# Three quarters of the query and key projection as products beside the gate's, the tokens' normalising on POOL, and a new issue table

## The chip, the core and the metric

The kernel runs on one core of one Trainium2 chip, in one launch. The metric is the device time of that core in microseconds (us), a median over runs. The core's engines are named as the profile names them: PE (TensorE matmul; PEld is its weight load), DVE (VectorE), ACT (ScalarE), POOL (GpSimd) and SP (SyncE, which here only issues DMAs).

## The reference

What is computed is a layer norm, an attention of 32 heads of width 16 without a mask, and a SwiGLU block whose output, through a SiLU, gates the attention's output; all in float32, 2048 tokens of width 512, inner width 1792.

```python
x = A_x                                     # [1, 2048, 512]
xn = _layernorm(x, axis=-1)
s = _A_ref(xn, A_wqkv, A_wo)                # qkv = xn @ wqkv; softmax(q k^T / 4) v per head; @ wo
g = _silu(_B_ref(xn, B_w1, B_w3, B_w2))     # (_silu(xn @ w1) * (xn @ w3)) @ w2
return x + s * g
```

## The kernel before

**Products in three parts.** A product in float32 precision is made of fp32r matmuls: each operand is split into a rounded high part and a rest (names ending in `h` and `l`), and three matmuls (l by h, h by l, h by h; `split3`, or `three` in the gate) are summed in PSUM. With a contraction of 512 in four slices of 128 rows (`KC`), one product of 128 by 512 outputs is 12 matmuls.

**Stage 1, the prologue** (L433 to L629). The 16 tiles of 128 tokens are normalised (`spread`: statistics on DVE and a power on POOL; `norm`: one DVE instruction), transposed on PE (`transposed`) and split by ACT and DVE into `xts`, four blocks of 512 tokens. Per block the kernel computes all eight row blocks of q and k (128 rows each: eight heads' worth; row blocks 0 to 3 are q, 4 to 7 are k), splits them (ACT copies the high part `sh`, DVE subtracts to `sl`) and stores them to DRAM (`qk`), and computes v for its four token tiles (`token_values`). For the first pair of heads, slices of k and q are loaded back into `ks` and `qs` and the first 64 maxima are taken between the products (`beside`, from a hand-written table `groups`). The normalised blocks 0 to 2 are stored to DRAM (`xt`) for the gate; block 3 stays in SBUF.

**Stage 2, the attention with the gate beside it.** The 16 pairs of heads are done in halves of 1024 queries, so 32 phases of 16 chunks (128 keys each). Four kinds of PE work are mixed:

- `m` (L403): scores of 128 queries by 512 keys for the row maxima, a matmul of 62 rows; DVE reduces it (L405). They run one phase ahead.
- `e` (L643): scores of 128 keys by 512 queries with the maximum already subtracted through two more rows; ACT takes the exponential into one of 23 `pt` tiles (L646).
- `f` (L877): the gate's products, each matmul cut into two halves of 64 rows. `m`, `e` and `f` thus all use half of the array's rows, and two of them run side by side, in two lanes.
- `pv` (L659): the values of one chunk, four matmuls side by side in column groups of the array, float32, eight records in the trace.

When a phase's maxima are complete, `max_rows` reduces and transposes them and writes them as two rows into `qs` through DMAs (L430); the phase's `e` can begin when these have landed.

**The order** of the PE work in stage 2 is the string `ORDER_OF_ISSUE`: a lower-case or capital letter is a half matmul in lane 0 or 1 (`f`, `s` for e, `m`), `v` or `r` is a chunk of values, `o` a step of the output projection. What cannot be issued at its letter by a planner (`Model`, times in us) is issued late. Weights of the gate come as `units` of 128 by 512 (`Weights`): a load into `wr`, then two POOL instructions that split it (L335, L336). SP issues all DMAs, in program order.

**Stage 3**, the output projection (`o`), begins beside the last two phases and ends the kernel.

Of the kernel before, what the change touches and what calls it, by code (L numbers as in the profile page):

```python
# [9 lines left out]
F32 = mybir.dt.float32  # L10
# [24 lines left out]
COLS = (2, 1, 0)  # L35
# [17 lines left out]
    "MffSMfSffSMfMfSffSMffSffMfsMfsMffSfsFFmFFsfMsfFmFsFFmFfSmFfFmfMFfmMvvsMSmfFFfsFfMFsFfmSfFsFmFFsfMsfF"  # L53
    "mFFffMMffMMfmMvvvMssSmFfFfFfMFsFfmSfFsFmFsFfMsfFFmSfFMffMSffsMvMsMffSfFfSFmSfFfMsfFSmFfSfFmFsFmFsFfF"
    "mFMfSfmSvMmmSmSvvMssSMmvmSFsFmFsFsFmsFFmFffFmFSfmFFfmSvfMfSfMSffSMfMfSfrMsmMsSvFmMsmMFmvvsMfSmFfFfSf"
    "MSffFmSfSfFmFsfFMFsFfmfFFMffSffMSffSfMsFFfmFsFFmsFFfmFsFmFsFMfFfMfMfmSvmSmMmFFvvMsSsmMvSmFmFssMvsMMm"
    "mSvvSmfSfMSffFfMSffMfSfFmFsFMffSsFFfmFFffMSffMfsFFFmsFsFFfmsFfFMsfFFmSfmFFfMffSMmvvmSMsMsvMmFsSmsFvm"
    "SMmMmvvRFsmFFsFmFsFsmFFffSfMfSfMfSfFFmfSffMSffMMsvmMMssSvmSFmsFfFSfFmfSFfMsFfFsMsFFfmSFffMsfFMFffMfS"
    "sMvSmMmFsFsvsMFmFsSmvSmmMmSvvmSmSmSvSmFsfMfSfFfMfSfMfSFfMfsFMffSsFFfmFFffMfSfMfsFFFmsfFFsFmFsFfMsFFf"
    "mSFfFmfMMffMsvvMmMmMmvvvMsfSfMfFSfFmSfFfSfMfFsFmfFFsfMFsMfFsFffMSfFmFfSffMSmvMssSMmvmSsSfMrSfMffSMff"  # L60
    "SfMfSfsFFmFsFfMsFFfmsFFMfsFsfFMfFsFmFsFmFsFfMfFsFFmsFFfMfMffSmSvmSSmMmvvSmMmsSvMffMMmmSvvfSfMfSfMSff"
    "MfSfSFfmFsFFfmFsFFmsFFmFfsFFmFfsFmFsFmfFSfFsFmFFfMfSfffMSMffSffMfSsMvvvvvFmFsFmsFFsmFsFFmFmFsFsFmFFf"
    "sFFfsfMfSFfMfSfMfFsFmFfFffMSfSffMfSMffMSffMSffMrvSmsMmMvvSmMsSmvsMFmFsFfsFfMFsFfmSFfsFmFsFFfmSFfFmsF"
    "sFfFmFsFfMfSFfmFFffMfSfMfSfSffMFsFfmFsFmFsFfFmFsFFmfFmFMfmMvvvmSSsmMvmSSmfSfMvSmmMsMvvmSfMfSfSfFFmfS"
    "FmFsFmFfSfMfFsFfSfMFsFfmFFffMfSfMfSffSfMFsfMfFsFmsFFfFmSfFmFsFsFfmFmFMmvvvmSSsmSvvRMsfSFfMfSfFmFsfFf"
    "SMsFFfmFsFfMsFffSMfSFfmFFffMSfffMSFfsfMsFfFmFsFmFsFFmFfsFmFSffMfFmMvvvMsfMfSFsFffMFsFfmSFfsFmFFsfMFs"
    "FfmSFfFmffMSfmMvvmSmSMsvvSmSsmMvmFFsFmFssFmFfFfSfMfSfMfSfFMfsfFMfSffSFmFFffMffMsFFfMfFsFfsFMFsFfmSFf"
    "FmsFfFmFfMfMmMvvvSmMsmMvvmSFmFsFfsFfMFsFfmSfFFsmFsFfMfSfFmSfFfMfSfMfSsvvvRsMfSFfMfsFFmFsfFFsMfSfFmfS"
    "fFMsfFfMSffSFmFFffMSffmFFsFmFsFsfFMFfsFmfSfFMsfFmFFffSMMsvvmSSssSvvSmSmSmvvMsmMmSvvMfSffMSfMffSfsFFm"
    "FFsfMsfFmFsFFmfFSmfFfFFfMfSfMfSfSffMsFFfmsFFmFsFFfmFsFFmsFFfMfMfMfmSvvMssMMmvvmSMfsFFffSfMfSfMfSfFmF"  # L70
    "sFMffSfFFsmFFsfMsFfMfSfmFFffSfMMmvvmSmSsMvvRSfMfSfMfSffMfSfSffMFsFfmSfFFmsFFsFfmFFsfMFsfFFmsFmFfSFfs"
    "FmFsFfMfSFfmSfsFfFfMfMMmvvvvMffSSmFmFfFfFsmFFssFFfMfFsFmFsFfFmSfFsFmFsFfMfSfFmsFfFMfSffMSfSfFfMffSmM"
    "vvmSMmmSvvfMfSfMSffMfSfsFFmsFfFMsfFmFSfFmFsFsfFMFsFfmSFfmFsFfFmFsMfFsFfFsFfMfSmMvvmSMmmSvvsMMmSsvvRf"
    "SfMfSfMfSfMfSffSfMFsfFmSFfFmsFsFFfmFFsFmsFfFmFFsmFFsFmFfsFsFfFSmvsMmMmSvvSmmMsMvvMsfSfMfFfSFmfSFfMsF"
    "ffSMfFsFmFsFmFsFFfmFMffSSmvvvMsfFmSfFsFfMsFFfmSfFfSmSfFfMSffFmSFfmfFFFfMffSMffSffMfSsFfFmFFsfMsFFfmF"
# [72 lines left out]
def kernel(ctx: ExitStack, tc: tile.TileContext, x, wqkv, wo, w1, w3, w2, out):  # L148
# [163 lines left out]
    class Weights:  # L312
# [37 lines left out]
        def next(self):  # L350

            i = self.taken
            self.taken += 1
            self.pump()
            return i, self.parts.pop(i)

    wts = Weights()
    for b in range(TB):
        for hf in range(HF):
            for f in range(hf * FH, (hf + 1) * FH):  # L360
                for w in (w1, w3):
                    wts.units.append(w[:, f * P:(f + 1) * P].rearrange("(k p) f -> p k f", p=P))
# [1000 lines left out]
```

## Time and profile before

| | us |
|---|---|
| median of 3 runs (lowest to highest) | 1720.81 (1720.58 to 1721.6) |
| the profiled execution | 1719.59 |
| its span, first to last instruction | 1717.8 |
| PE busy, DVE busy, ACT busy, POOL busy | 1708.2, 1408.0, 1224.0, 765.5 |
| first `f` matmul (stage 2 begins) | 160.7 |
| last chunk of values begins (stage 3 alone from there) | 1694.8 |

The durations used are those of the profiled execution, which is 1.2 us under the median; 1.8 us of its time lie outside its span. Matmuls are pipelined, so PE's busy time says only that it had something in flight; the spacing of the matmuls' starts says how much it did.

### The profile page before, as it was taken

The page shows a single profiled execution, that of the slowest core. Times are in us where ns is not written, and L with a number is a line of the kernel's source. Part 1 is how long each engine was busy: PE and PEld are TensorE (multiplying, and loading weights), DVE is VectorE, ACT ScalarE, POOL GpSimd, SP SyncE. Part 2 cuts the span into 40 slices and gives each one's busy share as a digit, 9 for nine tenths or more (in the row PEclk, how much of TensorE's full clock was granted, in tenths as well). Part 3 has the DMA queues.
Part 4 walks back from the last instruction along what each step waited for, and adds up shares of the span by engine and source line. Part 5 has one row for each costly group of instructions (what it writes and reads, how often), then busy time and mean ns, then how long its engine had stood idle before and what let it go on. Part 6 is the DMA issues. An engine that isn't in the chain of part 4 may idle for free.

```text
span 1717.8 us, 35102 instructions
## 1 busy us (share of the span) xinstructions
PE 1708.2 (99%) x13188; PEld 1102.6 (64%) x13188; DVE 1408.0 (82%) x2343; ACT 1224.0 (71%) x2440; POOL 765.5 (45%) x791
## 2 busy tenths in 40 slices
PE   9999999999999999999999999999999999999998
PEld 7877565666666666666666666666666666665456
DVE  7566999889898888888898798887988878889636
ACT  4223777777877786877777877887778777877880
POOL 3102646065635662466355643555465525653011
PEclk9999999999999999999999999999999999999999
DMA  8656203042333212222423222131513312331264
GB/s 286 245 204 204 71 22 86 21 82 70 65 104 88 62 55 51 64 60 69 100 88 62 62 67 68 43 82 54 137 51 65 74 37 71 99 85 29 81 206 147
DMA packets 146794, 155.34 MB, mean 90 GB/s; under 512 B 42304, under 2 KB 100672, under 8 KB 143648
## 3 DMA queue, kind: packets, MB, share of 16 engines
q1 hardware_dynamic: 145760, 151.52, 32.4%
q8 instruction: 104, 1.70, 0.4%
q10 hardware_dynamic: 864, 1.57, 0.2%
q14 instruction: 66, 0.54, 0.1%
HBM read 107.97 MB, written 44.02 MB: 88 GB/s over the span
## 4 chain that ended last, share of the span: by engine, by line
PE 95%; issue 2%; DMA 2%; SPq 1%; DVE 0%; ACT 0%; POOL 0%; ACTq 0%; POOLq 0%; DVEq 0%
PE f L877 28%; PE pv L659 27%; PE m L403 17%; PE e L643 15%; PE m L522 2%; PE e L197 2%; PE e L201 2%; PE e L199 2%; PE m L495 0%; PE m L418 0%; DMA ovl<-o 0%; SPq L695 0%; DMA wr<-in_A_wqkv_dram 0%; DMA ovh<-o 0%; DMA inh<-in_A_x_dram 0%
## 5 line engine op out<-in xcount | busy, mean ns | idle before, releaser
L405 DVE TENSOR_REDUCE mp<-m 128x1 f32<-128x512 f32 x2048 | 1276.8, 684 | 174.6 <-PE m L403 103.6
L646 ACT ACTIVATE pt<-e 128x512 f32<-128x512 f32 x2048 | 1061.0, 612 | 260.7 <-PE e L643 139.1
L643 PE MATMUL e<-qs,ks 64*128 64x512 f32 x2048 | 726.4, 408 | 2.5 <-DMA qs<-ml 2.5
L403 PE MATMUL m<-ks,qs 62*128 62x512 f32 x2048 | 725.6, 415 | 0.0
L659 PE MATMUL pv<-pt,vt 128*17 128x512 f32 x4096 | 489.8, 595 | 0.0
L403 PEld LDWEIGHTS m<-ks,qs 62*128 62x128 f32 x2048 | 339.1, 184 | 146.9 <-ACT pt L646 34.6
L643 PEld LDWEIGHTS e<-qs,ks 64*128 64x128 f32 x2048 | 345.1, 184 | 120.5 <-issue 35.0
L659 PEld LDWEIGHTS pv<-pt,vt 128*17 128x17 f32 x4096 | 94.2, 96 | 235.9 <-issue 229.1
L877 PE MATMUL f<-xtl,wh 64*128 64x512 f32 x488 | 177.9, 391 | 0.0
L877 PE MATMUL f<-xth,wl 64*128 64x512 f32 x488 | 176.1, 393 | 0.0
L877 PE MATMUL f<-xth,wh 64*128 64x512 f32 x488 | 174.4, 391 | 0.0
L762 POOL TENSOR_TENSOR h<-g,h 128x512 f32<-128x512 f32 x56 | 72.1, 1288 | 228.2 <-ACT h L758 228.2
L877 PE MATMUL f<-wh,hs 64*128 64x512 f32 x496 | 157.8, 393 | 0.0
L877 PE MATMUL f<-xtl,xeh 64*128 64x512 f32 x408 | 148.7, 391 | 0.0
L877 PE MATMUL f<-xth,xel 64*128 64x512 f32 x408 | 143.4, 394 | 0.0
L877 PE MATMUL f<-xth,xeh 64*128 64x512 f32 x408 | 142.6, 392 | 0.0
L877 PE MATMUL f<-xeh,hs 64*128 64x512 f32 x400 | 127.1, 392 | 0.0
L336 POOL TENSOR_TENSOR wl<-wr,wh 128x512 fp32r<-128x512 f32 x92 | 118.5, 1288 | 7.7
L335 POOL TENSOR_SCALAR wh<-wr 128x512 fp32r<-128x512 f32 x92 | 57.1, 621 | 115.9 <-PE e L643 56.5
L336 POOL TENSOR_TENSOR xel<-wr,xeh 128x512 fp32r<-128x512 f32 x76 | 97.9, 1288 | 6.3
L796 POOL TENSOR_SCALAR th<-th 128x512 f32<-128x512 f32 x16 | 9.9, 619 | 187.5 <-ACT th L792 187.5
L877 PE MATMUL f<-wl,hs 64*128 64x512 f32 x248 | 92.3, 392 | 0.0
(179 smaller groups left out, 2071.0 us busy)
## 6 DMA issues: line engine op xcount, KB each, us to landing
wr<-in_B_w_dram SPq DMA_DIRECT2D x168, 256.0 KB
qs<-qk SPq DMA_DIRECT2D x186, 64.0 KB
ks<-qk SPq DMA_DIRECT2D x90, 128.0 KB
qk<-sh SPq DMA_DIRECT2D x32, 256.0 KB
qk<-sl SPq DMA_DIRECT2D x32, 256.0 KB
v<-vrow SPq DMA_DIRECT2D x16, 272.0 KB
xin<-in_A_x_dram SPq DMA_DIRECT2D x16, 256.0 KB
g<-part SPq DMA_DIRECT2D x16, 256.0 KB
```

The source lines that it names most:

```text
L197: nc.tensor.matmul(ps, lhs[1], rhs[0], start=first, stop=False)
L199: nc.tensor.matmul(ps, lhs[0], rhs[1], start=False, stop=False)
L201: nc.tensor.matmul(ps, lhs[0], rhs[0], start=False, stop=last)
L335: nc.gpsimd.tensor_scalar(hi, t, 1.0, 1.0, op0=ALU.mult, op1=ALU.mult)
L336: nc.gpsimd.tensor_sub(lo, t, raw(hi))
L403: nc.tensor.matmul(ps, qs[p % 2][64 * h:64 * h + KM, q0:q0 + P], ks[p % 2][64 * h:64 * h + KM, c * 512:(c + 1) * 512], start=True, stop=True)
L405: nc.vector.reduce_max(mp[p, half][:, h, qt, c:c + 1], ps, axis=AX.X)
L643: nc.tensor.matmul(ps, ks[p % 2][64 * h:64 * h + KR, k * P:(k + 1) * P], qs[p % 2][64 * h:64 * h + KR, q0:q0 + 512], start=True, stop=True)
L646: done = nc.scalar.activation(pt, ps, AF.Exp, scale=DH ** -0.5)
L659: nc.tensor.matmul(pv[32 * j:32 * j + VW, :], vt[2 * p // GH][:, key, 2 * p % GH + j % 2, :], pt, start=key < 2 if last else k == 0, stop= ...
L762: nc.gpsimd.tensor_mul(h2, g, h2)
L877: nc.tensor.matmul(ps, left[r], right[r], start=starts and lane == 0, stop=ends and lane == 1)
```

## The change

Of the 32 products of the q and k projection (eight row blocks by four blocks of tokens), the prologue keeps the eight of row blocks 0 and 4, the first eight heads (`token_rows`). The other 24 become products of the gate's list: `rows_here` puts a pair of them (k, then q) ahead of gate products 0, 2 and 5 and behind the last down product of the first half (`hf == 0`) of the first three token blocks of the gate. Their tokens are the gate's current block, or another block fetched again from `xt` in DRAM into the tile `rows2` (`fetch_tokens`, `some_tokens`). Their weights are 24 more `units`, split by POOL. Their output is copied by ACT, split by POOL instead of DVE (`projected`), and stored by SP. A chunk that will need rows not yet stored is held back (`NEED`).

In the prologue, the normalising instruction of tiles 2 to 15 moves from DVE to POOL; the stores of v and of the high parts of q and k move from SP's queue to ACT's; block 3 is stored to `xt` too; the memsets stand in other places; the table `groups` is new, and 12 of the 16 last early maxima are in two groups of six. The last steps of the first phase's maxima (transposing them and writing them to `qs`) move out of the prologue into stage 2, which now begins with `m` and `f` work alone.

```diff
+    def room_between(n, hf):
+        return {0: (0, 2, 5, FH), 1: ()}[hf] if n < KC - 1 else ()
...
-            nc.sync.dma_start(v_d[t], vrow[t % 2].rearrange("p h d -> p (h d)"))
+            nc.scalar.dma_start(v_d[t], vrow[t % 2].rearrange("p h d -> p (h d)"))
...
-            nc.vector.tensor_scalar(xn, xin[t], mv[:, 0:1], rs, op0=ALU.subtract, op1=ALU.mult)
+            (nc.vector if t < 2 else nc.gpsimd).tensor_scalar(xn, xin[t], mv[:, 0:1], rs, op0=ALU.subtract, op1=ALU.mult)
...
+        def token_rows(b, c):
+            hi, lo = xts[b]
+            rbk = KC * c
+            ps = bank("e")
+            for k in range(KC):
+                run(split3(ps, [w[:, k, :] for w in wqk[c]], (hi[:, k, :], lo[:, k, :]), k == 0, k == KC - 1))
...
+            nc.scalar.copy(sh, ps)
+            nc.vector.tensor_sub(sl, ps, raw(sh))
+            cols = slice(b * 512, (b + 1) * 512)
+            nc.scalar.dma_start(raw(qk_d[rbk][0])[:, cols], raw(sh))
+            nc.sync.dma_start(raw(qk_d[rbk][1])[:, cols], raw(sl))
+
+        def more_tokens(n):
+            if n < NT:
+                transposed(n, xn.pop(n))
+                if n + 4 < NT:
+                    load_x(n + 4)
+                if n + 2 < NT:
+                    xn[n + 2] = norm(n + 2)
+
         for b in range(TB):
+            cols = slice(b * 512, (b + 1) * 512)
+            for s in range(2):
+                nc.sync.dma_start(raw(xt_d[b][s]), raw(xts[b][s]).rearrange("p k t -> p (k t)"))
+            token_rows(b, 1)
+            if b == TB - 1:
+                load_k(0, cols)
+                wts.start()
+            beside(b, 0)
+            more_tokens(4 * b + 4)
+            if b == 0:
+                nc.gpsimd.memset(*next(blank))
+                nc.gpsimd.memset(*next(blank))
+                more_tokens(5)
+            token_rows(b, 0)
...
+            beside(b, 1)
+            more_tokens(4 * b + (5 if b else 6))
+            if b == 0:
+                nc.gpsimd.memset(*next(blank))
+                nc.gpsimd.memset(*next(blank))
+                more_tokens(7)
+                load_q(0, 0, cols)
+                continue
+            for i in range(TB):
+                run(token_values(b, i))
...
+                beside(b, 2 + i)
+                if i < 2:
+                    more_tokens(4 * b + 6 + i)
...
+        def projected(ps, i, rbk, b):
+            flush(i - 1)
...
+            nc.scalar.copy(c, ps)
...
+                nc.gpsimd.tensor_scalar(sh.bitcast(F32R), c, 1.0, 1.0, op0=ALU.mult, op1=ALU.mult)
+                nc.gpsimd.tensor_sub(c, c, sh)
...
+                    nc.sync.dma_start(raw(qk_d[rbk][s])[:, b * 512:(b + 1) * 512], v)
...
+                def rows_here():
+                    t = rest.pop(0)
+                    src = xt if t == b else rows2
+                    for c in (1, 0):
+                        some_tokens()
+                        i, w = wts.next()
+                        mms = [m for k in range(KC) for m in three([v[:, k, :] for v in w], [v[:, k, :] for v in src])]
...
-    ready = {0: 0.5}
+    ready = {}
...
-    rows, outs = [], []
+    rows, outs = [[2.0, first_rows, 2, 0]], []
```

The table grows from 8617 to 9194 letters, 576 of them more `f` and `F`; one row of it before and one now:

```diff
-    "MffSMfSffSMfMfSffSMffSffMfsMfsMffSfsFFmFFsfMsfFmFsFFmFfSmFfFmfMFfmMvvsMSmfFFfsFfMFsFfmSfFsFmFFsfMsfF"
+    "MfMfMffMMffMMffMffMffRfMffMfMffMmFfFFmFffFfFFfFFfFmFmFfffMffMffMfSFfFfsFFfFsfFFsmFFsFmFFffmFsFFmFsfF"
```

Counted over the whole order of PE, there are 4032 half matmuls `f` before and 4608 now, and 384 full matmuls of the q and k projection before (lines L197 to L201) and 96 now; `m`, `e` and the records of `pv` are 2048 each before and now. The values stand in runs of chunks with no other matmul between them: 259 runs before (85 of one chunk, 119 of two, 37 of three, 12 of four, 6 of five), 204 now (32, 82, 54, 26, 10).

On PE, in the third phase (`e` and `m` of the second and third pair of heads; `x4` at a `pv` row is one chunk), before:

```order
L659 MATMUL pv<-pt,vt 17x512 x4
L643 MATMUL e<-qs_132,ks_134 128x512
L403 MATMUL m<-ks_135,qs_133 128x512
L877 MATMUL f<-xth,wh_1929 128x512
L403 MATMUL m<-ks_135,qs_133 128x512
L877 MATMUL f<-xth,wl_1930 128x512
L643 MATMUL e<-qs_132,ks_134 128x512 x2
L403 MATMUL m<-ks_135,qs_133 128x512
L659 MATMUL pv<-pt,vt 17x512 x4
```

Single chunks stood there with a few half matmuls between them. On PE, in the third phase, now (`ovh` and `ovl` are the tile `rows2` with other tokens):

```order
L691 MATMUL pv<-pt,vt 17x512 x12
L675 MATMUL e<-qs_133,ks_135 128x512 x2
L976 MATMUL f<-ovh_141,wl_2386 128x512
L419 MATMUL m<-ks_135,qs_133 128x512 x2
L976 MATMUL f<-ovl_142,wh_2385 128x512
L419 MATMUL m<-ks_135,qs_133 128x512 x2
L691 MATMUL pv<-pt,vt 17x512 x12
```

Three chunks now stand in a run, and the halves between two such runs hold a projection's matmuls.

On POOL, in the prologue around the first memset of `ks` (`rs` is the power of a tile's statistics), before:

```order
L479 TENSOR_TENSOR rs<-ve,minus 128x1
L615 MEMSET rb 128x512
L479 TENSOR_TENSOR rs<-ve,minus 128x1
L615 MEMSET ks_135 128x2048
L479 TENSOR_TENSOR rs<-ve,minus 128x1
L615 MEMSET qs_132 128x2048
```

Each memset stood behind the power of one more tile. On POOL, in the same place, now (`xn` of token tiles 6, 7 and 8):

```order
L498 TENSOR_TENSOR rs<-ve,minus 128x1
L505 TENSOR_SCALAR xn<-xin_353,mv,rs 128x512 [waits DMAHW4_49,PE_49,Pool_49]
L632 MEMSET rb 128x512
L633 MEMSET ks_135 128x2048
L498 TENSOR_TENSOR rs<-ve,minus 128x1 [waits DVE_49]
L505 TENSOR_SCALAR xn<-xin_381,mv,rs 128x512 [waits DMAHW5_49,PE_49,Pool_49]
L498 TENSOR_TENSOR rs<-ve,minus 128x1 [waits DVE_49]
L505 TENSOR_SCALAR xn<-xin_425,mv,rs 128x512 [waits DMAHW6_49,PE_49,Pool_49]
L643 MEMSET qs_132 128x2048
```

The normalising of tile 7 now stands behind two memsets on POOL's queue, and tile 7 is the last of block 1.

On PE, where stage 2 begins (`wqh` and `xth` of the last `m` are the last product of v), before:

```order
L522 MATMUL m<-wqh_155,xth 128x512
L403 MATMUL m<-ks_134,qs_132 128x512
L877 MATMUL f<-xth,xel 128x512
L877 MATMUL f<-xtl,xeh 128x512
L643 MATMUL e<-qs_132,ks_134 128x512
L403 MATMUL m<-ks_134,qs_132 128x512
```

The first `e` stood fourth. On PE, in the same place, now, at the transposing of the first maxima:

```order
L419 MATMUL m<-ks_134,qs_132 128x512
L976 MATMUL f<-xtl,xeh 128x512
L976 MATMUL f<-xth,xeh 128x512
L434 MATMUL m<-ident,nm 16x128
L976 MATMUL f<-xth,xel 128x512
L419 MATMUL m<-ks_134,qs_132 128x512
```

Nine `m` and twelve `f` stand ahead of the transposing now, and the first `e` follows 43 half matmuls behind it (20 `m` and 44 `f` stand ahead of it in all).

360 lines of the change are left out of this document (194 added, 166 removed).

## The prediction

> **What bounds the kernel now.** I read the page first, its busy line and its chain, then the waits of PE.
>
> ```profile
> span 1717.8 us, 35102 instructions
> PE 1708.2 (99%) x13188; PEld 1102.6 (64%) x13188; DVE 1408.0 (82%) x2343; ACT 1224.0 (71%) x2440; POOL 765.5 (45%) x791
> PE 95%; issue 2%; DMA 2%; SPq 1%; DVE 0%; ACT 0%; POOL 0%; ACTq 0%; POOLq 0%; DVEq 0%
> PE e L643 <- DMA qs<-ml: 2.5, 1, 2.5
> ```
>
> PE carries 95% of the chain, and its list of waits (total, times, longest) is all but empty: its longest entry is one wait of 2.5 us, where stage 2 begins. A busy share of 99% would not prove that, since a matmul in flight counts as busy; the spacing of the starts does. So the kernel's time is the sum of what its PE instructions take, and a change is worth what it does to that sum, plus the waits it makes. Next I priced the kinds of PE work. A full matmul in the prologue, and four transposes, from PE's timeline (start, length):
>
> ```profile
> 20.73 0.39 PE L197 MATMUL e<-xeh,wql 128*128 128x512 f32 x1
> 23.22 0.40 PE L201 MATMUL e<-xeh,wqh 128*128 128x512 f32 x1
> 23.46 0.60 PE L495 MATMUL m<-ident,xn 128*128 128x128 f32 x4
> 23.81 0.48 PE L197 MATMUL e<-xeh,wql 128*128 128x512 f32 x1
> ```
>
> Twelve matmuls fill 20.73 to 23.46: 0.2275 us each. Runs of values, from the timeline of stage 2:
>
> ```profile
> 394.91 2.77 PE L659 MATMUL pv<-pt,vt 128*17 128x512 f32 x24
> 397.61 0.50 PE L403 MATMUL m<-ks,qs 62*128 62x512 f32 x1
> ...
> 402.81 0.50 PE L403 MATMUL m<-ks,qs 62*128 62x512 f32 x2
> 403.24 1.91 PE L659 MATMUL pv<-pt,vt 128*17 128x512 f32 x16
> 405.08 0.50 PE L403 MATMUL m<-ks,qs 62*128 62x512 f32 x1
> 405.09 0.50 PE L643 MATMUL e<-qs,ks 64*128 64x512 f32 x1
> 405.42 0.39 PE L403 MATMUL m<-ks,qs 62*128 62x512 f32 x1
> ```
>
> Three chunks (x24) take 2.70 to the next matmul, two (x16) take 1.84: 0.86 a chunk, and 0.12 at a run's end. Halves otherwise start every 0.12. Ahead of the run the gap from the second of the two `m` (0.50 less 0.39 after the first, 402.92) to 403.24 is 0.32, so 0.20 more; behind it a lane's second matmul comes after 0.34, 0.11 more than 0.23; both lanes start at once, 0.12 less. A run costs 0.31 beyond its chunks, whether it has one or five.
>
> The price of a pair of halves comes from one window of 100 us, PE's instructions by tile (`e`, `m`, `f`, `pv` in this order; the count in brackets):
>
> ```profile
> 300.00:400.00 100.00, 49.40 (x134) 1.00 0.26 56
> 300.00:400.00 100.00, 51.18 (x143) 1.00 0.26 56
> 300.00:400.00 100.00, 60.48 (x293) 1.00 0.26 56
> 300.00:400.00 100.00, 30.52 (x256) 1.00 0.26 56
> ```
>
> 570 halves are 285 pairs; 256 records are 32 chunks, in about 32 x 259/512 = 16.2 runs. (100 - 32 x 0.86 - 16.2 x 0.31) / 285 = 0.237 us a pair. The whole of stage 2 tests it: 4032 pairs x 0.237 + 512 x 0.86 + 259 x 0.31 = 1476, with some 45 for the output steps in it 1521, against 1535 from 160.7 to the last chunk's end. There is little idle time for work to fill.
>
> **The change part by part.**
>
> *Products moved.* 24 x 12 x 0.2275 = 65.5 us leave the prologue, 288 pairs x 0.237 = 68.3 enter stage 2: +2.8. Moved as such, they gain nothing.
>
> *Runs of values.* 259 become 204, chunks stay 512: -55 x 0.31 = -17.0. This is the term that carries the forecast. It holds only if a longer run doesn't wait for its exponentials; 12 and 20 `pt` tiles are read at once where 23 exist, but runs of three to five were there before without a wait in PE's list. Between 0.2 and 0.4 a run it is -11 to -22.
>
> *The end of block 0.* Here the new prologue has a hole. K, two transposes, Q and two transposes follow each other, then K of block 1, which needs tiles 6 and 7; before, 24 more matmuls stood between. The chain to tile 7, from rows of DVE, ACT, POOL:
>
> ```profile
> 24.14 0.59 ACT L498 CAST xth<-m 128x512 fp32r<-128x512 f32 x1
> 24.27 0.69 DVE L593 TENSOR_TENSOR sl<-e,sh 128x512 fp32r<-128x512 f32 x1 [1.13 <-ACT sh L592]
> 24.88 0.68 DVE L499 TENSOR_TENSOR xtl<-m,xth 128x512 fp32r<-128x512 f32 x1
> 25.48 0.68 DVE L473 BATCH_NORM_STATS2 st<-xin 128x6 f32<-128x512 f32 x1
> 26.41 0.15 DVE L477 TENSOR_SCALAR ve<-mv 128x1 f32<-128x1 f32 x1
> 26.71 0.55 POOL L479 TENSOR_TENSOR rs<-ve,minus 128x1 f32<-128x1 f32 x1 [5.42 <-DVE ve L477]
> 33.59 0.53 POOL L615 MEMSET rb<- 128x512 f32 x1
> 39.04 1.81 POOL L615 MEMSET ks<- 128x2048 f32 x1
> L335 POOL TENSOR_SCALAR wh<-wr 128x512 fp32r<-128x512 f32 x92 | 57.1, 621 | 115.9 <-PE e L643 56.5
> L336 POOL TENSOR_TENSOR wl<-wr,wh 128x512 fp32r<-128x512 f32 x92 | 118.5, 1288 | 7.7
> ```
>
> Up to 24.9 the new kernel is as the old. ACT's own store issue (0.3 to 0.4) delays the rest: statistics of tile 6 at 25.8, its power at 27.0. Normalising on POOL has no row; it has one tensor input like L335 (0.62), the two-input L336 (1.29) is the other end, and I take 0.62: done at 28.2. Then the memsets, 0.53 and 1.81 (30.4), the power (31.0), the normalising of tile 7 (31.6). Its transposing, ACT's copy (0.6) and DVE's rest (0.7) let the second matmul of K follow at 33.9. Without the wait it would stand at 20.73 + 2 x 2.73 + 4 x 0.35 + 0.35 = 27.95. So PE loses 5.9 (4.5 if DVE gets to the statistics without the delays, 8 at 1.29 a normalising). For normalising the Trainium skill, GPSIMD Engine Reference, section 4.1, calls one-input work on GpSimd roughly line-rate, which speaks for the lower price.
>
> PE is idle there in pieces of about 1.3, 3.1 and 1.5 us. The first transposes of the program show what PE does after idleness:
>
> ```profile
> 1.36 4.71 PE L465 MATMUL pv<-ident 128*128 128x128 f32 x22 [1.36 <-POOL minus L460]
> ```
>
> 0.214 us each against 0.0875 at 23.46. After the wait of 2.5 us at 163.99 the spacing was at once 0.23, so I add nothing. The Trainium skill, TensorE: Matmul & The Clock Gate, Part 1, says that an idle window of about 3.4 us halves the clock until a busy window has passed. By that rule the hole may cost up to 1.7 more (half of 3.4), and the sum below would be 1715.2.
>
> *The start of stage 2.* The wait at its first `e`, 2.94 behind the matmul ahead of it where 0.12 is usual, goes: -2.8.
>
> ```profile
> 161.05 0.39 PE L877 MATMUL f<-xtl,xeh 64*128 64x512 f32 x1
> 163.99 0.47 PE L643 MATMUL e<-qs,ks 64*128 64x512 f32 x1 [2.55 <-DMA qs<-ml]
> 162.09 0.64 SPq L430 DMA_DIRECT2D qs<-ml  x1
> 164.73 17.95 DVE L405 TENSOR_REDUCE mp<-m 128x1 f32<-128x512 f32 x29 [2.80 <-PE m L403]
> 180.00:200.00 20.00, 20.00 (x166) 11.80 (x158) 18.99 (x32) 14.84 (x30) 14.23 (x15) 1.00 0.16 44
> ```
>
> DVE is late next. A reduction takes 17.95 / 29 = 0.62. The last six early maxima stand 2.7 + 0.7 us ahead of stage 2, so DVE begins it about half a microsecond late and then has 20 `m` ahead of the first `e` and the rest of the maxima (`ml`, 0.3): 12.7 us of reductions beside 64 halves, 7.7 us of PE. With seven PSUM banks, two held by `f`, some five `m` may be open: PE reaches the first `e` about 10.1 us after stage 2 begins instead of 7.8, 2.3 late. The DMAs of `qs` (last one issued about 8 us in, landed 1.9 later by 162.09 and 163.99) end at the same time. -2.8 + 2.3 = -0.5 (-2.8 to +3).
>
> *Slices of k and q in the prologue.* Before `m` of a new block can run, K and Q go out and come back:
>
> ```profile
> 48.11 2.95 SPq L391 DMA_DIRECT2D qs<-qk  x6
> 51.10 2.74 SPq L382 DMA_DIRECT2D ks<-qk  x6
> 27.12 1.24 SPq L440 DMA_DIRECT2D xin<-in_A_x_dram  x1
> q1 hardware_dynamic: 20320, 38.69, 68.6%
> ```
>
> Copy and rest 1.5, store landed about 2 later, six loads issued in 2.7, landed 2 later: 8.3 us. In block 3 PE has Q, a v product and two groups of `m`, about 7 us, before it needs them. I take +1.5 for the three places (0 to 6).
>
> *What else moves, off the path.* POOL gets 24 x 2 x (0.62 + 1.29) = 92 us more in stage 2:
>
> ```profile
> 400.00:600.00 200.00, 200.00 (x1652) 128.29 (x1651) 171.94 (x287) 153.66 (x307) 110.33 (x112) 1.00 0.30 76
> ```
>
> It is busy 110 of 200 there, ACT (24 copies of 0.6 more) 154; DMA 0.30, with 9 refills of `rows2` and 48 stores more. PE covers them; if a refill came late, its landing of about 2 us would show at each of nine places. Costed at nothing, 0 to 6 in the range. DVE's 24 subtractions and 14 normalisings leave an engine that nobody waits for.
>
> Sum: 2.8 - 17.0 + 5.9 - 0.5 + 1.5 = -7.3. The profiled execution took 1719.6: 1712.3. The median of the runs is 1.2 above it, so I forecast 1713.5.
>
> **Rivals.**
>
> *B, the hole closes.* If tile 7 is ready earlier (statistics not behind the subtraction, DMA quieter so that DVE runs ahead) and the start of stage 2 doesn't wait for DVE: -7.3 - 5.9 - 2.3 - 1.5 = -17.0, 1703.8. For it: stores leave SP's queue, loads come earlier. Against it: the memsets stand in POOL's order. 0.17.
>
> *C, longer runs wait.* A run of three needs 12 exponentials finished, at 0.5 to 0.6 us of ACT each. If each of the 55 merged runs waits half of its 0.31, 8.5 come back: 1722.0, no change. Against it: ACT is busy 77% and PE's list holds no wait for `pt` in stage 2. 0.15.
>
> *D, slower: SP's queue bounds the prologue.* Per block it issues about 20 DMAs, in order, each waiting for earlier ones. At 0.45 they take 9 us; at 1.24, as behind the two `xt` stores at 27.12, 25 us, where a block has about 20 us of PE work. The moved bytes speak for it: 38.7 MB took 68.6% of 165 us; without 12.6 + 1.5 and with 2.1 more, 26.7 MB take 78 us of about 100. If issue takes 1.24 throughout, 5 us in each of three blocks are lost: +15, 1728.5. It decides from 0.85 us an issue on the mean, where the 7.3 are gone. Against it: 1.2 lasted only some 8 us behind each pair of `xt` stores, and 24 stores leave this queue. The Trainium skill, DMA: Bandwidth & Descriptors, section "Issuing engines are not separate DMA queues", says that another issuing engine saves only issue time, not transfer time; that leaves D its bytes. 0.13.
>
> **How the numbers follow.** My forecast's case (0.55) spans 1706 to 1720 by the bounds above. B ends at 1703.8, C at 1722, D beyond. The range 1702 to 1725 leaves out most of D and little else. A change under 0.2% (3.4 us) could hardly be told from none. Faster: 0.52 of the forecast's case and 0.17, 0.69. Within: 0.03 and 0.12 of C, 0.15. Slower: 0.03 of C and 0.13, 0.16.
>
> **What would show it.** Stage 2 begins near 102 us with an idle PE near 28 to 34 us, of 5 to 6 in all, released by `xn` on POOL. A window of 100 us holds more `f` and fewer runs of `pv` at the same price of a pair; no PE wait for `pt`. The first `e` comes about 10 us after the first `f`. I am wrong if PE waits for `rows2`, `wr` or `pt` in stage 2, if the waits in the prologue exceed 10 us, or if runs of values cost by the chunk and not by the run.

## The result and the profile after

The changed kernel took 1729.51 us (median of four runs, 1728.48 to 1733.52), the kernel before 1720.69 beside it: a ratio of 1.0054 with an interval of 1.0037 to 1.0072. It is slower by 8.8 us; the forecast was 1713.5 (1702 to 1725). The profiled execution took 1728.9.

First the span, the chain's shares by engine, and PE's list of waits (total, times, longest):

```profile
span 1727.1 us, 35869 instructions
PE 88%; issue 6%; POOL 2%; DMA 1%; DVE 1%; SPq 0%; ACT 0%; ACTq 0%; POOLq 0%
PE m L514 <- POOL xn L505: 7.8, 5, 3.8
PE m L419 <- DMA qs<-qk: 5.2, 1, 5.2
PE m L419 <- DMA ks<-qk: 1.4, 2, 1.0
PE e L675 <- DMA qs<-ml: 1.3, 1, 1.3
```

POOL has come into the chain, and where the longest entry of the list was one wait of 2.5 us, these four lines now hold 15.7. (The share of issue is 6% in the fastest run below too, so it doesn't mark the loss.) All of these waits are ahead of 131 us. In stage 2 behind them PE has no wait for `pt`, `rows2` or `wr`. The same 100 us as before by tile (`e`, `m`, `f`, `pv`):

```profile
300.00:400.00 100.00, 47.93 (x131) 1.00 0.33 76
300.00:400.00 100.00, 48.93 (x139) 1.00 0.33 76
300.00:400.00 100.00, 62.33 (x309) 1.00 0.33 76
300.00:400.00 100.00, 30.00 (x256) 1.00 0.33 76
```

It holds 579 halves where there were 570, beside the same 32 chunks, in about 204/16 = 12.75 runs: (100 - 32 x 0.86 - 12.75 x 0.31) / 289.5 = 0.237 a pair, the price of before. From its first matmul to the last chunk stage 2 went from 1534.1 to 1587.6 us, 53.5 more; the prediction's terms make 68.3 - 17.0 - 0.5 = 50.8.

Most of the loss lies in the prologue, at two places. K and Q are the two products that the prologue keeps for each block of tokens. The end of block 0 on PE (start, length), and the same time on POOL:

```profile
28.43 0.39 PE L205 MATMUL e<-xeh,wqh 128*128 128x512 f32 x1
31.48 1.11 PE L514 MATMUL m<-ident,xn 128*128 128x128 f32 x4 [2.66 <-POOL xn L505]
36.40 1.11 PE L514 MATMUL m<-ident,xn 128*128 128x128 f32 x4 [3.81 <-POOL xn L505]
38.19 0.79 PE L201 MATMUL e<-xth,wkl 128*128 128x512 f32 x1 [0.68 <-ACT xth L517]
38.92 0.80 PE L203 MATMUL e<-xtl,wkh 128*128 128x512 f32 x1
39.51 0.63 PE L205 MATMUL e<-xth,wkh 128*128 128x512 f32 x1
39.94 0.63 PE L201 MATMUL e<-xth,wkl 128*128 128x512 f32 x1
```

```profile
29.35 2.08 POOL L505 TENSOR_SCALAR xn<-xin,mv,rs 128x512 f32<-128x512 f32 x1
31.37 0.53 POOL L632 MEMSET rb<- 128x512 f32 x1
31.84 1.80 POOL L633 MEMSET ks<- 128x2048 f32 x1
33.60 0.56 POOL L498 TENSOR_TENSOR rs<-ve,minus 128x1 f32<-128x1 f32 x1
34.27 2.08 POOL L505 TENSOR_SCALAR xn<-xin,mv,rs 128x512 f32<-128x512 f32 x1
```

A normalising took 2.08 on POOL, where the prediction had 0.62 with 1.29 as its other end. POOL runs without a gap from 29.35 to 36.3, tile 7 last, and the second matmul of K of block 1 stands at 38.92 instead of the forecast 33.9. Behind it matmuls follow each other after 0.43 us, not 0.23. The windows show why (the column behind POOL's is the granted clock):

```profile
30.00:40.00 10.00, 4.04 (x12) 2.61 (x13) 4.09 (x11) 1.17 (x2) 9.79 (x8) 0.55 0.41 134
40.00:50.00 10.00, 9.51 (x36) 7.04 (x35) 4.09 (x8) 1.94 (x4) 7.53 (x6) 0.77 0.38 132
110.00:120.00 10.00, 4.82 (x23) 4.09 (x23) 4.08 (x8) 0.90 (x3) 0.97 (x2) 0.82 0.77 185
```

Taken in windows of half a microsecond, the clock was half from 31.0 to 44.6 and again from 116.3 to 123.1. The second time comes from the second place, the start of stage 2. PE's last matmul of the prologue and its first of stage 2, and SP's issues ahead of it (start, time over all of the group's issues):

```profile
111.99 0.39 PE L541 MATMUL m<-wvh,xth 128*128 128x512 f32 x1
117.56 0.76 PE L419 MATMUL m<-ks,qs 62*128 62x512 f32 x1 [5.18 <-DMA qs<-qk]
```

```profile
99.48 0.95 SPq L325 DMA_DIRECT2D wr<-in_A_wqkv_dram  x2
100.47 0.51 SPq L325 DMA_DIRECT2D wr<-in_B_w_dram  x1
101.08 0.45 SPq L610 DMA_DIRECT2D qk<-sl  x1
105.50 3.40 SPq L398 DMA_DIRECT2D ks<-qk  x6
108.94 6.70 SPq L407 DMA_DIRECT2D qs<-qk  x6
115.68 0.42 SPq L325 DMA_DIRECT2D wr<-in_B_w_dram  x1
```

The first `m` needs the six slices of q. Ahead of them in SP's queue stand three loads of weights, the store of Q's rest and six loads of the next pair's k, which nobody needs for tens of microseconds. SP itself stood 4.0 us ahead of the first of those six and 3.0 within the loads of q, by the profile for stores of v (which this change moved to ACT's queue). Why a load of k or q waits for a store of v no run shows.

So the 16.6 us between the sum's 1712.3 and this execution are: block 0, 38.92 - 33.9 = 5.0; half clock from 39.5 to 44.6, about 2.5 (ten matmuls 0.2 longer each, four transposes 0.35 together, one more matmul 0.16); the wait at stage 2's start 5.57 - 0.3 = 5.3; the rest of the prologue (117.6 against 160.7 - 65.5 + 5.9 + 1.5 = 102.6, less these) 2.2; stage 2, 53.5 - 50.8 = 2.7, as much as the first `e` was late (at 130.37 it stood 12.8 behind the first `m`, where the prediction had 10.1); the tail behind the last chunk -1.1.

### The profile page after: what moved, and what is told of

The parts are those of the page before. It is cut to its first block, busy times and chain, and to the rows that moved or that the text cites. A ratio compares the mean times of both kernels' runs of the same rounds, so it can differ in the third digit from the quotient of the medians.

```text
span 1727.1 us, 35869 instructions
## 1 busy us (share of the span) xinstructions
PE 1702.8 (99%) x13476; PEld 1133.3 (66%) x13476; DVE 1375.0 (80%) x2299; ACT 1221.4 (71%) x2434; POOL 882.8 (51%) x901
## 2 busy tenths in 40 slices
DMA packets 170028, 181.07 MB, mean 105 GB/s; under 512 B 43776, under 2 KB 115456, under 8 KB 166624
## 4 chain that ended last, share of the span: by engine, by line
PE 88%; issue 6%; POOL 2%; DMA 1%; DVE 1%; SPq 0%; ACT 0%; ACTq 0%; POOLq 0%
PE f L976 31%; PE pv L691 25%; PE m L419 16%; PE e L675 14%; PE m L541 1%; POOL xn L505 1%; DVE mp L421 1%; DMA ovh<-o 0%; PE m L434 0%; POOL rs L498 0%; PE e L201 0%; DMA wl<-o 0%; PE e L203 0%; PE e L205 0%; DMA wr<-in_A_wqkv_dram 0%
## 5 line engine op out<-in xcount | busy, mean ns | idle before, releaser
L419 PE MATMUL m<-ks,qs 62*128 62x512 f32 x2048 | 743.5, 413 | 7.1 <-DMA qs<-qk 5.2
L675 PE MATMUL e<-qs,ks 64*128 64x512 f32 x2048 | 739.2, 406 | 1.3 <-DMA qs<-ml 1.3
L691 PE MATMUL pv<-pt,vt 128*17 128x512 f32 x4096 | 479.1, 594 | 0.0
L419 PEld LDWEIGHTS m<-ks,qs 62*128 62x128 f32 x2048 | 349.9, 185 | 128.1 <-issue 46.0
L976 PE MATMUL f<-xtl,xeh 64*128 64x512 f32 x448 | 164.3, 393 | 0.0
L976 PE MATMUL f<-xth,xeh 64*128 64x512 f32 x448 | 161.7, 394 | 0.0
L976 PE MATMUL f<-xth,xel 64*128 64x512 f32 x448 | 160.4, 395 | 0.0
L340 POOL TENSOR_TENSOR wl<-wr,wh 128x512 fp32r<-128x512 f32 x105 | 135.3, 1289 | 8.8
L340 POOL TENSOR_TENSOR xel<-wr,xeh 128x512 fp32r<-128x512 f32 x87 | 112.1, 1288 | 7.3
L339 POOL TENSOR_SCALAR xeh<-wr 128x512 fp32r<-128x512 f32 x87 | 53.8, 618 | 104.2 <-PE f L976 53.4
```

Source lines behind the costliest of these rows:

```text
L339: nc.gpsimd.tensor_scalar(hi, t, 1.0, 1.0, op0=ALU.mult, op1=ALU.mult)
L340: nc.gpsimd.tensor_sub(lo, t, raw(hi))
L419: nc.tensor.matmul(ps, qs[p % 2][64 * h:64 * h + KM, q0:q0 + P], ks[p % 2][64 * h:64 * h + KM, c * 512:(c + 1) * 512], start=True, stop=True)
L675: nc.tensor.matmul(ps, ks[p % 2][64 * h:64 * h + KR, k * P:(k + 1) * P], qs[p % 2][64 * h:64 * h + KR, q0:q0 + 512], start=True, stop=True)
L691: nc.tensor.matmul(pv[32 * j:32 * j + VW, :], vt[2 * p // GH][:, key, 2 * p % GH + j % 2, :], pt, start=key < 2 if last else k == 0, stop= ...
L976: nc.tensor.matmul(ps, left[r], right[r], start=starts and lane == 0, stop=ends and lane == 1)
```

## The experiments

Each ratio is against the kernel before, run on the same chip at the same time (its medians were 1720.6 to 1721.0). The theory: stage 2 gains as forecast, and the prologue loses it through POOL's normalising, the half clock behind it, and the order of SP's queue. The rivals: the transfers bound the smaller prologue, or runs of values don't carry the price that the prediction gave them.

**The price of a run of values.** Thirty long runs cut in two in the table, as `vvvMs` to `vvMsv`.

> The changed kernel with 30 of its runs of three or more chunks of values cut in two, by one step of the table moved behind two halves: 233 or 234 runs instead of 204 over the same 512 chunks, and all else the same. By the prediction's price of 0.31 us a run 9.2 us more, 1738.7 (0.2 to 0.4: 6 to 12 more). Rival (values cost by the chunk, and longer runs wait for exponentials as much as they save): no change, 1729.5.

Measured: 1740.35, ratio 1.0113 (1.0099 to 1.0126). That is 10.8 us over the changed kernel, 0.36 a run (about 0.2 to 0.5 by the two intervals) where 0.31 was forecast. PE's list has no wait for exponentials with the runs split or whole, so values cost by the run, and the 55 merged runs were worth about 17 to 20 us. The rival by the chunk is out.

**The price of the normalising.** First the prediction's own chain, with its own price. This kernel leaves out the mean and the scale of tiles 2 to 15, so it prices the operation and is no repair:

```diff
-            (nc.vector if t < 2 else nc.gpsimd).tensor_scalar(xn, xin[t], mv[:, 0:1], rs, op0=ALU.subtract, op1=ALU.mult)
+            if t < 2:
+                nc.vector.tensor_scalar(xn, xin[t], mv[:, 0:1], rs, op0=ALU.subtract, op1=ALU.mult)
+            else:
+                nc.gpsimd.tensor_scalar(xn, xin[t], 1.0, 1.0, op0=ALU.mult, op1=ALU.mult)
```

> The changed kernel with the normalising on POOL of tiles 2 to 15 done by constants in place of each row's mean and scale, so these tiles are left as they are read; the power is still taken ahead of each. A POOL operation with two constants takes 0.62 us, the price that the prediction put on the normalising, where it took 2.08. So this run has the prediction's own chain: its step said that tile 7 is normalised at 31.6, the second matmul of K of block 1 stands at 33.9 and PE loses 5.9. Theory P (that price was the error): it stands at about 34 instead of 38.9, the waits for tiles 2 and 3 go (1.9), and some of the half clock: 1721 to 1724. Rival (another wait takes its place): 1727 to 1730.

Measured: 1725.92, 1.0032 (1.0021 to 1.0042). POOL and PE:

```profile
31.02 0.61 POOL L508 TENSOR_SCALAR xn<-xin 128x512 f32<-128x512 f32 x1
```

```profile
31.69 1.11 PE L517 MATMUL m<-ident,xn 128*128 128x128 f32 x4 [2.66 <-POOL xn L508]
34.20 0.79 PE L203 MATMUL e<-xtl,wkh 128*128 128x512 f32 x1
```

The second matmul of K stands at 34.20; the prediction worked out 33.9. The chain was right and the price wrong. By medians that is worth 3.6 us of the 16.0 by which the forecast missed. The clock halved here too, from 31.4 to 38.2: four transposes took 1.11 where 0.60 is usual, and the eleven matmuls from the second of K on took 4.48 where 2.50 is.

Then that part of the change alone, in the kernel before (its L486 on POOL from tile 2 on):

> The kernel before with one part of the change alone: tokens from tile 2 on normalised on POOL. There 24 more matmuls a block stand between the transposes. Theory P (POOL's price matters only where the moved matmuls no longer cover it): 2 us more for tiles 2 and 3 and 1 to 3 more at the end of block 0, 1722 to 1725. Rival (each of 14 normalisings costs PE its 1.5 us more): 1742. Other rival (all of it is covered, and the whole loss comes from the smaller prologue): 1720.7.

Measured: 1721.9, 1.0005 (0.9996 to 1.0014): no difference. Where the moved matmuls still stand between the transposes, 2.08 us on POOL cost nothing that can be measured. It takes the smaller prologue to expose them.

**The clock.** 20 transposes of the identity ahead of tile 6's and 32 ahead of tile 7's.

> The changed kernel with 20 transposes of the identity ahead of tile 6's and 32 ahead of tile 7's, whose result nobody reads; the memset of the bank that they write stands behind them. Nothing that PE waits for is earlier, so this takes away the idleness of PE and leaves the waits. At full clock they take 52 x 0.0875 = 4.6 us of about 6.5 us of waiting. Theory P with the clock's share: no half clock from 31 to 44.6, matmuls of block 1 at 0.23 from the start, 2.7 us less or a little more: 1726.5. Rival (the clock doesn't hang on PE's idleness here): half clock stays, the transposes take 0.21 each, 11 us in place of 6.5, and the time is 1729.5 to 1734.

Measured: 1726.69, 1.0037 (1.0024 to 1.0049), as forecast, though the interval touches that of the changed kernel. The windows decide:

```profile
30.00:40.00 10.00, 7.84 (x59) 6.63 (x58) 4.40 (x12) 1.17 (x2) 9.79 (x8) 1.00 0.43 150
40.00:50.00 10.00, 9.91 (x48) 7.03 (x46) 7.18 (x14) 2.87 (x5) 8.22 (x6) 1.00 0.66 257
```

The clock is 1.00 where it was 0.55 and 0.77, and the second matmul of K stands at 38.88, where it stood at 38.92: the waits are unchanged and the clock alone is mended. So work on PE, even work that nobody reads, keeps the clock up there. Elsewhere it dropped in this run too: from 60.2 to 63.6 behind a wait of 1.5 us for slices of k, where the changed kernel's clock stayed full, and from 114.8 to 121.7 at the start of stage 2.

**Normalising on DVE again, and the memsets.** Three runs: `nc.vector` for every tile; POOL kept and the four memsets behind tile 9's normalising; POOL kept and the memsets ahead of block 0's K.

> The changed kernel with every token normalised on DVE again (0.55 us each), all else as changed. Theory P (the loss is idle time of PE at the end of block 0, made by POOL's 2.08 us a normalising, and half clock behind it): the waits for xn on POOL (7.8 us in 5 places) shrink to what the two memsets ahead of tile 7's power leave, about 2.5 us; the second matmul of K of block 1 stands near 33.5 instead of 38.9, no record of half clock from 31 to 44.6 (13 matmuls at 0.43 instead of 0.23, 2.7 us): 8 us less in all, 1721.5. Rival Q (SP's queue and the DMAs bound the prologue, and PE's waits only move): the start of stage 2 stays near 117.6 and the time within 3 us of 1729.5.

> The changed kernel, normalising on POOL, with the four memsets of block 0 (0.53, and three of 1.80) behind tile 9's normalising instead of two ahead of tile 7's statistics and two behind. Theory P: tile 7 is 2.3 us earlier (34.1 instead of 36.4) and PE's idle time shorter by as much; whether the clock halves is open, since the two waits left are about 2.7 and 1.5 us: 1725 to 1727. Rival (POOL's memsets fill time in which POOL would wait for DVE's statistics anyway): tile 7 stays near 36 and the time at 1729.5.

> The changed kernel, normalising on POOL, with the four memsets ahead of block 0's K, where POOL waited 3.95 us for DVE, so that neither tile 7's normalising nor the loads of q stand behind them. Theory P: T7 at 34.1 as with the memsets late, without the 3.8 us that PE then waited for the slices of q at 47.9: 1727. Half clock stays for a while, since the waits at tiles 6 and 7 stay at 2.7 and 1.5 us or so. If the memsets run into tile 6's power instead (5.9 us of memsets in 4 us of room), T6 comes up to 2 us later and nothing is won: 1729.

Measured: 1737.33, 1.0100 (1.0084 to 1.0115); 1732.93, 1.0065 (1.0053 to 1.0078); 1728.73, 1.0047 (1.0034 to 1.0061). None of them wins. With the memsets late tile 7 came at 33.7, and then PE waited 3.8 for slices of q, whose loads left SP at 44.08, when their memset had ended; with them early tile 6 waited 4.4 for POOL. With DVE the time rose, which no theory had. DVE and POOL in that run:

```profile
27.90 2.46 DVE L505 TENSOR_SCALAR xn<-xin,mv,rs 128x512 f32<-128x512 f32 x1 [0.73 <-POOL rs L498]
...
36.17 3.74 DVE L505 TENSOR_SCALAR xn<-xin,mv,rs 128x512 f32<-128x512 f32 x1 [0.73 <-POOL rs L498]
```

```profile
27.81 0.53 POOL L632 MEMSET rb<- 128x512 f32 x1
28.27 1.81 POOL L633 MEMSET ks<- 128x2048 f32 x1
...
36.08 1.80 POOL L643 MEMSET qs<- 128x2048 f32 x1
37.82 1.81 POOL L644 MEMSET qs<- 128x2048 f32 x1
```

DVE's 0.55 became 2.46 and 3.74, each ending within 0.3 us of the end of POOL's memsets (30.08 and 39.63). DVE's next instruction, the rest of tile 7, came that much later, and PE waited 4.7 for it. The trace of before has this too, three times, without harm to PE; beside the memset at 39.04 that the prediction quotes stands

```profile
39.13 2.00 DVE L486 TENSOR_SCALAR xn<-xin,mv,rs 128x512 f32<-128x512 f32 x1 [0.73 <-POOL rs L479]
```

A first repair of everything ran into the same thing. It had DVE's normalising, the four memsets ahead of block 0's K, tile 3's values behind Q, and SP's order of the next experiment:

> The changed kernel with four repairs: normalising on DVE, the four memsets ahead of block 0's K (so that DVE's normalisings don't wait for a power behind a memset, as they did when only the engine was changed back), the twelve matmuls of tile 3's values held back into the hole ahead of tile 6's transposes, and the order of SP's DMAs as in the run on that. Theory P: of 9 us of idleness and 2.7 of half clock at the end of block 0 about 2 are left, and 5 to 8 go at the start of stage 2: 1711 (1706 to 1716), faster than both kernels. Rival Q (the DMAs bound the smaller prologue): the prologue keeps its length and the waits move on: 1722 to 1728.

Measured: 1734.65, 1.0078 (1.0064 to 1.0092), above what the theory and the rival had. Tile 5's normalising, beside 5.8 us of memsets on POOL, took 5.96.

**SP's queue at the start of stage 2.** In three steps, each with the one before. The first (the loads of q straight behind the store of Q, then weights, then k at the prologue's end):

```diff
             if b == TB - 1:
                 load_k(0, cols)
-                wts.start()
...
-                load_k(1)
+                load_q(0, 1)
+                wts.start()
...
                 if i == 0 and b == TB - 1:
-                    load_q(0, 1)
                     wts.pump(KC)
...
+        load_k(1)
         load_v(1)
```

The second step, and the third:

```diff
-                nc.sync.dma_start(raw(qs[p % 2])[r:r + 1, c], raw(v)[8 * h:8 * h + 8, :])
+                (nc.sync if p + half else nc.scalar).dma_start(raw(qs[p % 2])[r:r + 1, c], raw(v)[8 * h:8 * h + 8, :])
```

```diff
-        load_k(1)
...
+        if count["S"] == 12:
+            load_k(1)
```

> The changed kernel with another order of SP's DMAs ahead of stage 2: the loads of the second half of q, for which stage 2's first m waits 5.2 us, straight behind the last store of Q; the three loads of raw weights behind them instead of ahead of that store; the loads of the next pair's k behind the prologue's last. Theory P (that wait is made by the order of the queue): stage 2 begins at 112.3 without half clock from 116 to 123, the first e is bound by DVE's maxima at about 125 instead of 130.4: 5 to 8 us less, 1723. Rival Q (the DMA engines are full, and the slices land no earlier): 1728 to 1729.5.

> The changed kernel with the start of stage 2 alone mended: SP's order, and the rows of maxima of the first phase on ACT's queue; normalising on POOL and memsets as changed. In the run of SP's order alone stage 2 began 5.7 us earlier and gave it all back at the first e, whose rows left SP 8.3 us after DVE had them (118.04 to 126.36). Theory: first e near 121.5 instead of 130.5, 9 us less: 1720 to 1721. Rival (the e's or the first values then wait for something else, weights or exponentials): 1726 to 1729.

> The changed kernel with the start of stage 2 mended further: SP's order and the rows of maxima on ACT's queue as in the run of the start, and the six loads of the second pair's k, which held SP from 106 to 114 us there, moved behind the twelfth exponential of stage 2. Theory (what each repair won was waited for at the next thing behind the weights and k in SP's queue, last at a copy of ACT that waits for a store of the moved products): the weights behind k are issued from 107 instead of 115, POOL splits them from 109 instead of 121 and stores the moved products' rows 6 to 8 us earlier, and the wait of 3.4 us for exponentials at the first values goes: 1724 to 1726. Rival (DMA bandwidth, not order): 1729 to 1732 with another wait in its place.

Measured: 1733.52, 1.0070 (1.0057 to 1.0083); 1731.05, 1.0066 (1.0053 to 1.0080); 1727.55, 1.0039 (1.0025 to 1.0053). The new order alone brought stage 2 to 111.85, and PE then stood at the first `e`:

```profile
130.50 0.76 PE L675 MATMUL e<-qs,ks 64*128 64x512 f32 x1 [6.49 <-DMA qs<-ml]
```

```profile
117.77 0.27 DVE L438 TENSOR_TENSOR ml<-m,mh 16x128 fp32r<-16x128 f32 x1
```

```profile
106.54 9.26 SPq L398 DMA_DIRECT2D ks<-qk  x6
116.33 0.38 SPq L390 DMA_DIRECT2D vt<-v  x1
116.80 3.16 SPq L325 DMA_DIRECT2D wr<-in_B_w_dram  x2
120.06 1.22 SPq L325 DMA_DIRECT2D wr<-in_A_wqkv_dram  x2
121.33 1.90 SPq L771 DMA_DIRECT2D ovh<-xt  x2
125.88 0.38 SPq L325 DMA_DIRECT2D wr<-in_B_w_dram  x1
126.36 0.80 SPq L446 DMA_DIRECT2D qs<-mh  x1
```

The maxima are ready at 118.0 and leave SP at 126.4, behind k and weights. With them on ACT's queue the first `e` came at 124.4, and the first run of values, begun at 132.4, then waited 3.4 in its middle for exponentials, because ACT, in order, stood at a copy into a buffer whose store of a moved product was behind weights in SP's queue:

```profile
137.43 0.59 ACT L808 COPY g<-f 128x512 f32<-128x512 f32 x1 [5.04 <-DMA qk<-ch]
```

Only with k out of the way too did that wait go: the second run of values began at 144.7, against 147.1 in the run before it and 146.7 in the changed kernel. It was the order: the same bytes are moved in all three. The whole loss of the start was not won back so.

**Both places.** The hole mended (DVE normalises; the memset of q that block 0 needs stands early, the others in block 1; tiles 6 and 7 are normalised ahead of K), alone and with the first two steps of the start:

```diff
+            if t == 1:
+                nc.gpsimd.memset(raw(qs[0]), 0.0)
...
+        of = [spread(t) for t in (6, 7)]
+        xn.update((t, norm(t, *of[t - 6])) for t in (6, 7))
```

> The changed kernel with the hole alone mended, as in the run of both; the start of stage 2 as changed. Theory: 13.7 us go in block 0, and the wait for the slice of q at stage 2's start stays at about 5, with SP's rows of maxima behind it: 1716 (1713 to 1720). If what is won in block 0 is waited for again at the start of stage 2 (its loads don't come earlier): 1725 to 1729.

> The changed kernel with both places mended. Hole: DVE normalises, the statistics of tiles 6 and 7 and their normalisings stand ahead of block 0's K, those of tiles 8 and 9 behind tile 7's transposes, and no memset on POOL stands where a DVE normalising would run beside it (in the runs with DVE's normalising, one of 0.55 us took 2.46, 3.74 and 5.96, ending each time with POOL's memset). Start: SP's order as in the run on it, and the four rows of maxima that the first e waits for go out on ACT's queue instead of SP's, where they stood 8.3 us behind weights. Theory: the second matmul of K of block 1 near 30 instead of 38.9 and no half clock there (9 + 2.8 + 1.9 for tiles 2 and 3); the first e about 10 us after the first f: 1707 (1703 to 1713), faster than both kernels. Rival Q (the DMA engines bound the smaller prologue): the first e stays within 5 us of 130 and the time above 1722.

Measured: 1728.76, 1.0050 (1.0037 to 1.0063); 1726.49, 1.0033 (1.0022 to 1.0045). K's second matmul came at 32.5 in both, 6.4 earlier than in the changed kernel. Alone that bought nothing: with the start as it was, PE waited 2.2 in block 3, at half clock behind it, and 5.0 at stage 2, which began at 117.6 as before the repair. With the start's two steps it began at 108.7 and lost 3.5 at the first values, as above; the first `e` came at 120.9, so the rival's mechanism is out there, though the time lies where it had it. One memset still met DVE in both: tile 3's normalising took 3.27 beside it, and its transposes waited 1.8.

The same with the third step, and block 0 mended further (q cleared at the very start, tile 3's values behind tile 7's transposes, the first slices of q loaded ahead of tokens, and four early maxima one group later):

> The start as in the run beside it, and block 0's hole mended further: DVE normalises, slices of q cleared by POOL at the very start, the twelve matmuls of tile 3's values behind tile 7's transposes, the loads of the first slices of q ahead of those of tokens, and the first early maxima one group later. The run with both places mended still lost 2.2 us at tile 3, 1.9 at K of block 1, 3.5 at the slices of q, 5 at the first values, of 8 above the kernel before. Theory (all of the loss sits in these waits): 1714 to 1718, faster than both. Rival (the smaller prologue is bound by its transfers, and another wait comes up): 1722 to 1727.

Measured: 1722.91, 1.0013 (1.0004 to 1.0021). The hole is closed (K's second matmul at 29.2), and a new wait stands in block 1, where two memsets still met DVE. Moving them into stage 2, and then tiles 10 to 15 back to POOL:

> The run all_clear with the three remaining memsets of POOL moved out of block 1 to behind the first four weights' splitting of stage 2, and the loads that need them behind the twelfth exponential. In all_clear two normalisings of DVE took 2.46 and 2.00 in place of 0.55 beside these memsets; tile 9's transposes waited 2.7 us for DVE, and 1.3 and 0.6 us waits at maxima with half clock from 54 to 58 followed. Theory (DVE's normalising and POOL's memset exclude each other, and that is what the time went to): no DVE normalising over 0.6 us after tile 3's, 4 to 6 us less, 1717 to 1719, just faster than before. Rival (DVE, busy 9 of 10 us in block 1, is full anyway, and the wait stays without the memsets): 1721 to 1723.

> As memsets_out, and tiles 10 to 15 normalised on POOL, whose 2.08 us are covered there: six times 0.55 us leave DVE, which was busy 8.5 to 9.2 of each 10 us from 40 to 80. Theory (DVE's load bounds blocks 1 and 2 of the smaller prologue): another 1 to 3 us less, 1715 to 1718. Rival (POOL's power and normalising in a row come too late for tiles 10 and 11): 1718 to 1721.

Measured: 1721.93, 1.0004 (0.9995 to 1.0012); 1719.15, 0.9992 (0.9984 to 1.0001). Every DVE normalising from tile 4 on took 0.55 once no memset stood beside it. The step of 1.0 that moving them made is within the measurement and lies where the rival had it, so what the memsets of block 1 cost stays open; the two steps together are 3.8 us.

Last, the waits that this trace still named: loads of tiles 8 and 9 earlier, four early maxima moved from block 1 to block 3, and the row maxima (`R` in the table) after fewer maxima of stage 2 (six `m` stand ahead of the transposing in its trace, nine did in the changed kernel).

> memsets_out_mixed with the waits that its trace still shows taken out: the loads of tiles 8 and 9 are issued ahead of block 0's stores (tile 8's transposes waited 1.5 us, tile 9's 1.1), four early maxima of block 1 and their slices of k and q move to block 3 (waits of 2.3 and 1.3 us), and the row maxima of the first phase are turned after four new maxima of stage 2 instead of ten (the first e waited 0.6). Theory (each of these waits is on PE's path): 4 to 6 us less, 1714 to 1716, faster than the kernel before by 0.3%. Rival (DVE, at 8.5 to 9 of 10 us from 60 to 110, takes the moved maxima no faster, so they come back as waits in block 3): 1718 to 1720.

Measured: 1716.56, 0.9979 (0.9969 to 0.9988), just faster than the kernel before. Its span, and the first matmul of stage 2:

```profile
span 1714.0 us, 35869 instructions
```

```profile
101.53 0.50 PE L419 MATMUL m<-ks,qs 62*128 62x512 f32 x1
```

Stage 2 begins at 101.5, where the prediction expected it (102), with the changed kernel's 181.07 MB of transfers; so the transfers do not bound the smaller prologue at that length. What it still lacks of the sum, 3.4 us in this execution (3.1 by medians), lies in stage 2, which took 1590.5 from its first matmul to the last chunk, against 1584.9 in the sum; its start and its tail are 1.1 shorter each than there. From the first chunk to the last it took 1571.4, where the changed kernel took 1566.8, and no wait on PE's list accounts for that; it stays open.

## Why the prediction was wrong

*Right:* products moved and runs of values. Stage 2 came out at 53.5 for 50.8, a pair at 0.237, 0.36 a run by its own experiment. PE doesn't wait for `rows2`, `wr` or `pt` in it; POOL's and the DMAs' extra work are hidden there. Rival C fell with that.

*The end of block 0 failed by one price.* The prediction had no row for the normalising on POOL and took the nearest by its inputs, 0.62, bounded by 1.29. It was 2.08, outside the bounds. The 5.9 became 10.9 with the waits at tiles 2 and 3; the run with constants gave the prediction's chain to 0.3 us. The rows used had two constants; this instruction has a mean and a scale for each row, and no row bounded that. The Trainium skill, GPSIMD Engine Reference, section 4.1, whose one-input work at roughly line-rate was cited for the lower price, does not hold for this instruction here: 2.08 against 0.62 for the same 128 by 512.

*"I add nothing" for the clock failed, and not only because the waits grew.* The clock halved at 31.0, 2.2 us into the first wait, and cost about 2.5 at block 0. It halved at the prediction's own price too: in the run with constants PE's waits there were 1.05, 2.66 and 0.67 us, none longer than the forecast's 1.3, 3.1 and 1.5, and the half clock cost 4.48 - 2.50 = 2.0 in K alone. One wait of 2.5 without effect was no ground for a price of nothing. The warning that the prediction drew from the Trainium skill, TensorE: Matmul & The Clock Gate, Part 1, held, though the drop came after 2.2 us without work and not after a window of about 3.4. Its 1.7 was too small: in the changed kernel the clock stayed down for 13.6 us, not for one window.

*The start of stage 2 failed by an unread queue.* The prediction allowed 1.5 for slices in three places (6 at most) and counted 6.8 us from a store to its slices: store landed 2, six loads issued 2.7, landed 2. It did not list what stands ahead of `load_q(0, 1)` on SP. From the store of Q's rest (101.08) to the first `m` (117.56) it took 16.5, and PE, which had work for 11.3 of them, waited 5.2. In the new order the six loads of q were out 5.3 behind that store.

*The first `e` was mis-sized as well.* The -0.5 rests on 10.1 us from the first `m` to the first `e`; it was 12.8, and 12.0 at full clock with the start mended. So the half clock of 116.3 to 123.1 and the queue cost at most 0.8 there. 12.0 to 12.8 is near the 12.7 us of DVE's reductions that the prediction counted, as if none of them were covered; that this is the reason is argued, not shown.

*Rival D* named SP's queue and 1728.5, near the time, but its mechanism was another: 1.24 an issue in every block. What happened was one stretch in which the wrong loads came first. The six loads of q took 6.70 there, six of k 3.40; an issue of k took 0.42 at most, and the rest of q's time was waiting. Its time was near by luck.

*Rival B*, the hole closing by itself, had the memsets "in POOL's order" against it. That was so, and the memsets did more than that: with DVE's normalising put back, it waited for them.

The sum needed all its covers at once. Of the repairs made alone none brought the time below 1726, and with all of them and the four steps behind them (memsets, tiles 10 to 15, early maxima and loads) it came to 1716.6.

## What to carry to other kernels

When work is taken out from between the stages of a pipeline, price every instruction that it covered on the engine that will run it, with its own form of operands; a price from a row with other operands is a guess without bounds. List each in-order queue at the place that becomes critical, from the wait back, since a load that nobody needs yet costs as much as one that is late. And before crediting a removed wait, look what stands next in the queues: here two repairs in a row moved the wait and won nothing. A wait of 2 to 3 us can cost the clock as well, so price that too.

## What the runs showed of the hardware

- A normalising with a mean and a scale for each row takes 2.08 us on POOL for 128 by 512 (changed kernel), an operation with two constants 0.62 (0.61 in the run with constants); on DVE the normalising takes 0.55.
- DVE's normalising waits for the end of POOL's memset: 0.55 became 2.00 (kernel before, at 39.13), 2.46 and 3.74 (normalising on DVE), and 5.96 (first repair of everything); beside a split of weights on POOL it took 1.50 (kernel before, at 8.52). Other work of DVE kept its time beside a memset: reductions from PSUM 0.61, statistics 0.68 and rests 0.69 (changed kernel, at 38.78 and 33.25). That a memset waits for DVE no run shows. The Trainium skill, GPSIMD Engine Reference, section 1, says that POOL's SBUF interfaces are shared with VectorE, in contention with its two-port modes or with two inputs in SBUF. The traces agree that the two contend; whether this normalising runs in such a mode no run here shows.
- The granted clock halved 2.2 us into a wait of 2.66 us (changed kernel) and 2.4 into another of 2.66 (run with constants), not in a wait of 2.5 (kernel before). It stayed at half for 13.6, 6.8 (twice) and, in the run with the hole alone mended, 3.4 us (33.0 to 36.4): about whole multiples of 3.4.
- Splitting a run of values in two, with half matmuls between, cost 0.36 us, on the mean of 30.
